# Loading two small matrices with two transfers on one queue instead of five on two

## The chip, the cores and the metric

The kernel runs on one core of a Trainium2 chip. The metric is device microseconds for one execution; lower is better. Before the change, three timed runs took 223.18, 223.17 and 222.88 us (median 223.17).

## The reference

Two blocks are chained. The first is an attention with sketched features: for each of 4 batches and 4 heads, queries, keys and values are 1088 tokens by 32, and two sketch matrices S1 and S2 (8 x 32 each) make the features.

```python
def phi(x):
    a = np.einsum('rd,bhsd->bhsr', S1, x)
    b = np.einsum('rd,bhsd->bhsr', S2, x)
    return np.einsum('bhsi,bhsj->bhsij', a, b).reshape(*x.shape[:-1], r * r)
q_p, k_p = (phi(q), phi(k))
kv = np.einsum('bhsf,bhsd->bhfd', k_p, v)
num = np.einsum('bhsf,bhfd->bhsd', q_p, kv)
den = np.einsum('bhsf,bhf->bhs', q_p, np.sum(k_p, axis=2))[..., None] + 1e-06
x = num / den                      # then (B,H,S,D) -> (B,S,H*D)
```

The second block turns x into a phase, `theta = x @ w_theta`, mixes `x*cos(theta)` and `x*sin(theta)` along the tokens with two 1088 x 1088 matrices (w_tok_r, w_tok_i), adds x to get u, and returns `u + relu(u @ w_ch)`. S1, S2 and the w matrices arrive as 8-byte floats, which the kernel unpacks itself.

## The kernel before

**Stages.** Tokens lie in chunks of 128 partitions. Keys, queries and values of a batch are one tile each: 128 rows of 4608 bytes, 576 KB, loaded by one transfer on SyncE's queue (SP in the profile, `load`, line 677). For each batch the kernel forms sums of key products (`key_sums`: keys are split into a short rounded part, `hf`, and a rest; matrix products of both are summed on TensorE), key features and their products with the values (`kfeatures`), and a normalising chain (`chain`). For three of the four batches the sums also need a second copy of the keys (line 723, the tile that the profile also calls `big<-k_l`), onto which GpSimd's queue adds the rounded part by an accumulating transfer (`join`, line 398, `big<-hf`). The token mixing, in which w_tok's 17 slabs of 1088 KB come in one after another (line 649), fills most of the second half of the run.

In what follows k0, k1, q0, k2, kh1, q1, k3 are the first seven of these 576 KB loads in the order in which SP issues them: keys of batches 0 and 1, queries of batch 0, keys of batch 2, the second copy of batch 1's keys, queries of batch 1, keys of batch 3. "The first join" is the accumulating transfer onto kh1, and "the rest products" are the TensorE instructions that read its result.

**What sets the order.** The kernel records some thousand operations, each with its engine and its buffers, and issues them in one order written out as a table of numbers (`ORDER`, lines 29 to 67). Each engine executes its own in that order. TensorE's list holds a fixed number of dummy products on a tile `idle` (line 435, `spin`), so that it isn't idle while it waits.

**Completion semaphores.** The transfers that SP and ScalarE (ACT) issue take eight completion semaphores in turn, and a transfer whose turn comes round again waits until the one that held that semaphore eight places earlier has landed. The built program shows this as waits on DMAHW0 to DMAHW7: in the program before, k2 is the ninth such transfer and waits for k0.

**The small matrices.** S1 and S2, transposed, are one input `s_t` of 32 rows by 16 eight-byte words (128 bytes a row); S2 is also an input `s_2` of 8 rows by 32 words. They go to the tile `st` of 128 partitions, `s_t` four times, once for each head's 32 partitions. Line 455 issues one transfer per copy, two on ACT's queue (line 464) and two on SP's (line 465); line 457 brings `s_2`, on SP's queue. All of them wait for a memset of `st` on VectorE (DVE, line 463).

**Who needs them.** ACT makes the upper words (`sp<-st`, line 471) after it has squared and summed k0 (line 702). DVE unpacks the rest (lines 477 to 480), takes a maximum (line 513), and by way of TensorE and ACT (`scaled`, lines 525 to 527) gets the scaled matrices that it rounds (`rounded`, `s<-sm`). Between these steps DVE also works on the keys: the rounded part of k0 (`hf`, line 388), its rest (line 384), then the rounded part of k1, which the first join adds.

Of the kernel before, what the change touches and what calls it, by code (L numbers as in the profile page):

```python
# [26 lines left out]
TINY = 2.0**-60  # L27
UP = 256.0
ORDER = """
    0 1 36 12 13 4 10 11 139 14 54 58 59 39 55 15 16 5 60 8 140 61 62 63 64 65 66 67 68 69 56 85 19 133 17 152  # L30
    18 127 37 70 20 41 89 57 71 72 21 22 73 91 74 75 80 81 23 128 134 82 76 297 94 153 90 24 25 3 92 299 29 245
    238 239 93 249 83 129 154 130 26 300 135 155 77 95 298 96 42 97 98 131 136 99 100 101 78 40 180 181 156 86
    295 146 137 32 296 158 147 33 251 254 255 301 102 87 141 48 49 34 7 51 50 38 52 79 174 232 302 159 132 256
    252 138 113 114 103 104 105 115 106 107 108 109 110 111 193 197 53 142 44 160 175 112 88 143 118 176 119 332
    333 161 162 9 226 120 121 27 186 144 233 145 35 122 187 257 258 199 352 123 259 260 261 2 124 354 28 84 125
    262 305 177 182 183 303 273 6 165 250 148 149 30 227 150 335 253 126 167 43 334 188 347 274 275 189 221 412
    416 336 417 116 117 348 418 276 419 420 413 414 169 168 415 190 178 421 422 222 202 223 423 203 204 205 166
    206 173 207 315 424 304 208 311 45 425 327 194 151 224 228 263 426 427 306 353 240 316 184 264 265 47 428
    157 163 229 164 319 429 171 430 241 431 432 46 328 433 307 195 308 309 234 179 434 342 323 329 185 324 320
    441 310 321 322 191 448 266 267 268 192 269 270 437 312 31 438 200 330 435 442 271 436 443 230 444 445 439  # L40
    331 337 235 236 446 523 440 519 520 338 339 451 452 447 521 455 457 524 525 458 449 522 526 450 515 516 517
    209 382 198 231 201 242 518 527 246 172 464 463 459 460 461 465 528 529 466 530 456 247 453 454 237 248 243
    462 272 472 531 340 532 533 313 467 341 534 468 244 471 349 372 170 535 344 473 314 469 210 211 212 536 213
    474 214 215 216 217 537 480 544 373 374 343 345 218 219 220 481 482 538 540 539 545 541 546 547 548 542 551
    549 543 559 550 196 470 552 346 553 355 475 362 554 566 350 558 555 477 560 561 562 351 357 317 356 564 556
    568 563 483 569 567 476 278 557 358 359 570 363 484 574 576 485 279 565 280 479 478 572 577 629 630 631 571
    365 281 583 578 360 606 573 607 580 282 364 608 283 284 384 632 361 367 369 633 634 584 407 277 285 609 225
    610 611 368 486 318 579 392 383 366 370 371 286 660 661 662 409 656 663 657 658 659 288 408 652 653 385 375
    376 654 575 581 585 397 586 410 411 582 587 635 636 386 637 638 394 588 291 293 393 287 395 396 655 664 377
    378 380 379 381 289 290 612 398 589 590 591 592 487 387 400 388 390 402 294 639 665 666 667 668 488 640 403  # L50
    669 670 671 389 391 489 672 673 825 490 491 404 399 405 678 401 492 493 494 406 495 676 674 325 326 679 828
    496 497 503 718 719 720 509 675 721 714 715 716 717 710 711 712 292 823 713 824 677 680 857 641 853 822 722
    681 642 723 643 593 498 682 724 683 684 725 726 727 728 686 729 730 731 734 644 732 736 685 735 687 688 499
    500 689 693 695 691 737 645 613 614 615 616 617 618 619 620 696 646 594 690 701 733 621 738 739 827 740 692
    741 697 698 702 595 856 703 694 742 699 704 705 802 803 501 744 783 784 785 804 743 765 707 792 767 700 805
    806 807 756 786 787 788 768 758 706 769 708 747 770 749 793 808 759 760 750 510 504 826 751 794 795 809 796
    797 798 762 855 745 761 746 748 752 753 754 774 502 596 622 709 852 755 764 766 819 757 623 881 789 790 771
    763 820 839 772 840 773 851 841 842 829 843 879 821 914 511 512 810 799 844 845 848 882 791 868 869 513 846
    775 811 776 777 778 624 597 849 854 850 877 858 870 878 847 871 872 873 647 779 780 781 895 883 916 598 782
    880 896 884 859 860 897 625 915 874 919 875 626 505 898 899 861 900 901 902 903 506 507 815 862 863 876 904  # L60
    908 864 917 920 936 937 508 909 830 831 865 866 800 867 816 921 514 938 832 833 834 922 927 835 836 837 838
    939 599 923 924 926 940 928 929 953 930 627 918 952 801 600 941 601 885 628 925 886 887 888 889 890 891 892
    893 894 812 813 814 648 649 650 912 651 942 943 944 931 817 954 818 910 932 965 913 975 966 905 906 933 934
    948 602 935 603 955 956 957 604 605 949 958 945 959 960 950 946 961 962 963 947 976 977 978 979 907 964 985
    967 968 969 970 951 986 980 971 911 972 973 987 988 981 982 983 974 984 989 991 990 992 993 994 996 995 997
    998
"""
WARM = 0
FILL = 5.0
# [250 lines left out]
def kernel(  # L320
# [12 lines left out]
    B, _, NC, H, D = q.shape  # L333
    S, DM = out.shape[1], out.shape[2]
    R = s_2.shape[0]
# [34 lines left out]
    op, buf = L.op, L.buf  # L370
# [4 lines left out]
    V, A, G, T, SY = nc.vector, nc.scalar, nc.gpsimd, nc.tensor, nc.sync  # L375

    def fixed(shape, dt, name):
        b = Buf(None, shape, dt, name)
        n = math.prod(shape) * WORD[dt]
        b.ap = view(const.tile([P, (n + 3) // 4], F32, tag=name, name=name), shape, dt)  # L380
        return b

    def tt(eng, o, a, b, f):
        eng.tensor_tensor(out=o, in0=a, in1=b, op=f)  # L384

    def ts(o, a, s1, op0, s2=None, op1=None, eng=None):
        kw = {} if op1 is None else {"op1": op1}
        (eng or V).tensor_scalar(out=o, in0=a, scalar1=s1, scalar2=s2, op0=op0, **kw)  # L388

    def stt(o, a, s, b, op0, op1, eng=None):  # L390
        (eng or V).scalar_tensor_tensor(out=o, in0=a, scalar=s, in1=b, op0=op0, op1=op1)  # L391
# [8 lines left out]
    def vop(n, fn, w, r, two=False, lk=0):  # L400
        op("V", dve2(n) if two else dve(n), fn, w, r, lk=1 if two else lk)
# [46 lines left out]
    NS = 2 * R + D  # L448
    sp = fixed((2, NS), F32, "sp")
    wide = s_t.dtype != F32  # L450

    def read_heads(E, i0, i1):
        dst = st() if wide else sp()[:, 0]
        for i in range(i0, i1):
            E.dma_start(dst[i * D:(i + 1) * D, 0:2 * R], s_t.rearrange("d t r -> d (t r)"))
        if i1 == H:
            E.dma_start(dst[0:R, 2 * R:NS], s_2)

    if wide:
        st = fixed((NS,), I64, "st")  # L460
        y = fixed((NS,), I32, "sy")
        z = fixed((NS,), I32, "sz")
        op("V", 0.1, lambda: V.memset(st().bitcast(F32), 0.0), [st], [])
        op("A", 0.48 * 2, lambda: read_heads(A, 0, 2), [(st, 0)], [], fly=2.7)
        op("S", 0.5, lambda: read_heads(SY, 2, H), [(st, 1)], [], lk=3)

        def words():
            w = st().bitcast(I32).rearrange("p (n t) -> p n t", t=2)
            return w[:, :, 0], w[:, :, 1]

        op("A", 0.25, lambda: A.activation(sp()[:, 0], words()[1].bitcast(F32), AF.Prelu, scale=2.0**-112,
                                           alpha=-(2.0**32)), [(sp, 0)], [st])

        def unpack():
            wl = words()[0]
            x = sp()[:, 0].bitcast(I32)
            ts(x, x, 3, ALU.logical_shift_left)
            stt(x, wl, 29, x, ALU.logical_shift_right, ALU.bitwise_or)
            ts(y(), x, -(1 << 23), ALU.bitwise_and)
            ts(z(), wl, 0x1FFFFFFF, ALU.bitwise_and)  # L480

        op("V", 0.85, unpack, [(sp, 0), y, z], [st], lk=2)
        op("A", 0.25, lambda: A.activation(sp()[:, 1], z(), AF.Copy, scale=2.0**-52), [(sp, 1)], [z])
        vop(NS, lambda: tt(V, sp()[:, 1], sp()[:, 1], y().bitcast(F32), ALU.mult), [(sp, 1)], [y])
    else:
        op("V", 0.2, lambda: V.memset(sp(), 0.0), [sp], [])
        op("A", 0.4 * H + 0.4, lambda: read_heads(A, 0, H), [(sp, 0)], [], fly=2.0)

    def powers(mfn, m, n, name):

# [6 lines left out]
        def inv():  # L497
# [16 lines left out]
                                    op=ALU.max, apply_absolute_value=True), [m2], [(sp, 0)])  # L514
# [989 lines left out]
```

## Time and profile before

| | |
|---|---|
| median of three runs | 223.17 us (222.88 to 223.18) |
| profiled execution | 222.87 us |
| span in its profile (first to last instruction) | 221.1 us |
| TensorE busy | 212.9 us of the span (96%) |
| DVE, ACT, GpSimd busy | 164.4, 113.5, 43.1 us |
| granted TensorE clock | 1.000 |
| moved by DMA | 40.19 MB |

The page divides the span into slices and says how busy each engine was; "PE" is TensorE's products, "PEld" its weight loads. A line of the timeline gives the start, the time from the first start to the last end, the engine, the source line, what is written and read, how many instructions were merged, and in brackets how long the engine had been idle and who ended the idleness. SPq, ACTq and POOLq are the issuing of transfers, which isn't counted as busy time. The chain of waits follows the end of the run backwards, at each step to what released it.

### The profile page before, as it was taken

How to read it: one execution, taken by the hardware profiler on the slowest of the kernel's cores; microseconds unless marked ns; L12 is line 12 of the kernel's file. 1: busy time of each engine (PE TensorE's matmuls, PEld its weight loads, DVE VectorE, ACT ScalarE, POOL GpSimd, SP SyncE). 2: the span in 40 equal slices, each digit the busy share in tenths (PEclk: the TensorE clock that was granted, in tenths of full speed). 3: DMA queues.
4: the chain of work that ended last, by engine and by line, in shares of the span. 5: the costliest groups of instructions: out<-in, count | busy, mean ns of one | idle time of the engine just before them, and what ended most of it. 6: DMA issues, size and time to landing. Idle time of an engine off the chain costs nothing.

```text
span 221.1 us, 5087 instructions
## 1 busy us (share of the span) xinstructions
PE 212.9 (96%) x2065; PEld 160.7 (73%) x2065; DVE 164.4 (74%) x343; ACT 113.5 (51%) x232; POOL 43.1 (20%) x79
## 2 busy tenths in 40 slices
PE   7997899989999999999999999999999999999992
PEld 3786688867876666687666687669878778778791
DVE  1889788999898999999999959943699132237631
ACT  4779359889999799856671251358920000000000
POOL 1146523001000000101002560000244355130000
PEclk9999999999999999999999999999999999999999
DMA  5999999993617306959900993002099689962572
GB/s 161 359 402 356 403 423 359 426 388 104 231 31 249 129 8 217 354 233 335 313 6 8 177 165 62 0 3 36 9 185 173 107 146 152 171 93 44 87 114 56
DMA packets 27047, 40.19 MB, mean 182 GB/s; under 512 B 18320, under 2 KB 19344, under 8 KB 24848
## 3 DMA queue, kind: packets, MB, share of 16 engines
q1 hardware_dynamic: 22176, 30.29, 40.4%
q0 software_dynamic: 4752, 9.57, 24.4%
q8 instruction: 16, 0.26, 0.5%
q14 instruction: 7, 0.06, 0.1%
q10 hardware_dynamic: 96, 0.01, 0.0%
HBM read 28.07 MB, written 2.23 MB: 137 GB/s over the span
## 4 chain that ended last, share of the span: by engine, by line
PE 81%; DMA 11%; ACT 3%; SPq 2%; issue 1%; DVE 1%; ACTq 0%; POOLq 0%
PE ps L404 75%; DMA big<-k_l 5%; DMA big<-hf 5%; PE ps L1191 2%; PE ps L1158 2%; SPq L1286 2%; PE ps L1038 1%; ACT big L652 1%; PE ps L435 1%; DMA out<-g 1%; ACT big L650 0%; ACT big L1006 0%; ACT big L1041 0%; PE ps L795 0%; ACT g L1298 0%
## 5 line engine op out<-in xcount | busy, mean ns | idle before, releaser
L404 PE MATMUL ps<-big,zs 128*128 128x384 f32 (+4 forms) x366 | 101.9, 426 | 0.0
L404 PEld LDWEIGHTS ps<-big,zs 128*128 128x128 f32 x366 | 65.5, 190 | 26.8 <-DVE big L388 0.6
L1270 ACT COPY g<-ps 128x384 f32<-128x384 f32 (+1 forms) x6 | 2.8, 459 | 41.5 <-PE ps L404 41.5
L650 ACT ACTIVATE big<-zs 128x1088 f32<-128x1088 f32 x17 | 20.5, 1214 | 5.3 <-DMA zs<-w_tok 5.3
L384 DVE CUSTOM_DVE_ANT_0 big<-big,big 128x2176 uint16<-128x2176 uint16 x17 | 21.8, 1287 | 0.4
L652 ACT ACTIVATE big<-zs 128x1088 int32<-128x1088 uint32 (+1 forms) x18 | 20.8, 1171 | 0.4 <-DVE big L384 0.2
L391 DVE SCALAR_TENSOR_TENSOR big<-ps,even,big 128x256 f32<-128x256 f32 (+1 forms) x10 | 4.9, 492 | 13.5 <-PE ps L404 13.5
L1331 POOL DMA_DIRECT2D big<-big x8 | 9.5, 1502 | 27.2 <-DVE big L384 15.0
L1331 POOL DMA_DIRECT2D big<-zs x8 | 7.7, 1063 | 36.8 <-PE ps L404 33.9
L404 PE MATMUL ps<-big,big 128*32 128x32 f32 (+2 forms) x320 | 13.7, 220 | 0.8 <-DMA big<-hf 0.8
L384 DVE TENSOR_TENSOR zs<-ps,g 128x768 f32<-128x768 f32 (+2 forms) x20 | 12.3, 627 | 2.9 <-PE ps L1191 1.7
L404 PE MATMUL ps<-mf,big 128*128 128x96 f32 x72 | 14.4, 295 | 0.0
L404 PEld LDWEIGHTS <-hf 128*32 128x32 bf16 (+1 forms) x252 | 10.8, 99 | 4.3 <-issue 2.3
L435 PE MATMUL ps<-idle 128*128 128x384 bf16 x46 | 11.7, 383 | 1.3 <-POOL idle L437 1.3
L404 PEld LDWEIGHTS ps<-big,big 128*32 128x32 f32 (+1 forms) x320 | 10.1, 117 | 3.9 <-DMA big<-hf 1.1
L1298 ACT COPY g<-ps 128x128 f32<-128x128 f32 x2 | 0.5, 265 | 22.9 <-DMA out<-g 22.2
L388 DVE TENSOR_SCALAR big<-big 128x1088 int32<-128x1088 int32 x17 | 12.0, 720 | 0.0
L404 PEld LDWEIGHTS ps<-w,big 128*128 128x128 f32 x76 | 10.1, 191 | 2.2 <-ACT g L1298 1.2
L404 PE MATMUL ps<-w,big 128*128 128x128 f32 x76 | 10.8, 278 | 0.8 <-ACT g L1298 0.8
L384 DVE TENSOR_TENSOR g<-lv 128x768 f32<-128x768 f32 x12 | 11.0, 952 | 0.6 <-PE ps L1158 0.6
L391 DVE SCALAR_TENSOR_TENSOR g<-g,ps 128x384 f32<-128x384 f32 x12 | 6.5, 545 | 6.1 <-ACT g L1200 6.1
L404 PEld LDWEIGHTS ps<-mf,big 128*128 128x128 f32 x72 | 10.9, 191 | 0.0
(195 smaller groups left out, 388.9 us busy)
## 6 DMA issues: line engine op xcount, KB each, us to landing
zs<-w_tok SPq DMA_DIRECT2D x17, 1088.0 KB, 6.6
big<-k_l SPq DMA_DIRECT2D x7, 576.0 KB, 6.8
big<-q_l SPq DMA_DIRECT2D x4, 576.0 KB, 11.0
big<-v_l SPq DMA_DIRECT2D x4, 576.0 KB, 15.0
big<-big POOLq DMA_DIRECT2D x8, 272.0 KB, 4.8
big<-zs POOLq DMA_DIRECT2D x8, 272.0 KB, 4.1
zs<-big POOLq DMA_DIRECT2D x8, 272.0 KB, 5.2
big<-hf POOLq DMA_DIRECT2D x3, 576.0 KB, 10.4
```

Of the source, the lines that this page charges most:

```text
L384: eng.tensor_tensor(out=o, in0=a, in1=b, op=f)
L388: (eng or V).tensor_scalar(out=o, in0=a, scalar1=s1, scalar2=s2, op0=op0, **kw)
L391: (eng or V).scalar_tensor_tensor(out=o, in0=a, scalar=s, in1=b, op0=op0, op1=op1)
L404: T.matmul(o, lhs, rhs, start=start, stop=stop, skip_group_check=True)
L435: T.matmul(nowhere(), idle()[:, 0:P], idle(), start=True, stop=True, skip_group_check=True)
L650: op("A", 0.22 + n * 0.0009, lambda: A.activation(dfn(), words_of(raw(), n)[1].bitcast(F32), AF.Prelu, scale=2.0**-112, alpha=-(2.0**32)), ...
L652: op("A", 0.22 + n * 0.0009, lambda: A.activation(stp(), words_of(raw(), n)[0].bitcast(U32), AF.Copy, scale=2.0**-29), [stp], [raw])
L1158: T.transpose(tr()[:, i * P:(i + 1) * P], qp()[:, i * H + 2 * n:i * H + 2 * n + 2].rearrange("p h i j -> p (h i j)"), ident())
L1191: T.transpose(x()[:, i], xs()[:, off + i * P:off + (i + 1) * P], ident())
L1270: op("A", act(w), lambda: A.copy(u(), yp()[:, :w]), [uT], [yp])
L1286: SY.dma_start(out[b, t0 - o:t0 + w, f * SQ:(f + 1) * SQ].rearrange("(c j) i -> j c i", j=SQ), ot()[f * SQ:(f + 1) * SQ, :o + w].rearrange ...
L1331: op("G", 1.05, lambda i=i: G.dma_start(dst[0](i), x[0](i), accum_op=ALU.add), [dst[1](i)], [x[1](i)], chan=ADD_FLY3)
```

## The change

Both inputs come on ACT's queue: one transfer writes all 128 partitions from `s_t`, with a source pattern that goes over the 32 rows four times, and one brings `s_2`. SP issues none of them. The recorded operations are one fewer, so the table of the order is numbered anew.

```diff
-    def read_heads(E, i0, i1):
+    def read_small():
         dst = st() if wide else sp()[:, 0]
-        for i in range(i0, i1):
-            E.dma_start(dst[i * D:(i + 1) * D, 0:2 * R], s_t.rearrange("d t r -> d (t r)"))
-        if i1 == H:
-            E.dma_start(dst[0:R, 2 * R:NS], s_2)
+        A.dma_start(dst[:, 0:2 * R],
+                    s_t.rearrange("d t r -> d (t r)").partition_broadcast(H))
+        A.dma_start(dst[0:R, 2 * R:NS], s_2)
...
-        op("A", 0.48 * 2, lambda: read_heads(A, 0, 2), [(st, 0)], [], fly=2.7)
-        op("S", 0.5, lambda: read_heads(SY, 2, H), [(st, 1)], [], lk=3)
+        op("A", 0.48 * 2, read_small, [st], [], fly=3.0)
```

In the built programs, each engine's list of instructions is the same before and after, in the same order and with the same number of dummy products, but for these transfers: ACT issues two before and two after, SP issues three fewer. What SP's and ACT's transfers wait for follows the new turns of the eight completion semaphores: k2, kh1 and q1 wait for none, and k3 is the first that waits for k0.

## Prediction

> **What bounds the kernel now.** I read the chain of waits first. Its pieces in order of time (start, us, what):
>
> ```profile
> 0.73 3.90 DMA big<-k_l
> 4.63 0.02 issue
> 4.64 0.33 SPq L677
> 4.97 0.04 issue
> 5.02 7.90 DMA big<-k_l
> ...
> 13.51 10.94 DMA big<-hf
> 24.45 0.04 issue
> 24.49 2.31 PE ps L404 x66
> ...
> 165.14 44.37 PE ps L404 x188
> ```
>
> From 24.49 us on nearly all of it is TensorE work, which the change leaves as it is. Before that it is a row of transfers: k0; then SP, which may issue k2 only when k0 has landed; kh1, issued right after; then the first join, which needs kh1. So the stage to look at is the first 24.5 us, and the question is how much sooner the rest products can start. The list of waits from 60 us on shows TensorE waiting 1.2 us in all, at the very end: what is gained at 24.49 us should last.
>
> The timeline of the first 14 us shows what the edit touches (start, duration, engine, line):
>
> ```profile
> 0.98 0.86 ACTq L455 DMA_DIRECT2D st<-s_t  x2
> 1.16 0.88 SPq L455 DMA_DIRECT2D st<-s_t  x2
> 2.08 0.37 SPq L457 DMA_DIRECT2D st<-s  x1
> 2.49 0.35 SPq L677 DMA_DIRECT2D big<-k_l  x1
> 5.81 0.23 ACT L471 ACTIVATE sp<-st 128x48 f32<-128x48 f32 x1
> 7.64 1.17 ACT L702 ACTIVATE big<-big 128x1152 f32<-128x1152 f32 x1 [0.77 <-DMA big<-k_l]
> 12.37 0.19 DVE L388 TENSOR_SCALAR s<-sm 128x48 f32<-128x48 f32 x1 [0.44 <-ACT sm L527]
> ```
>
> SP spends 1.16 to 2.49 us on small transfers, so k1 is issued at 2.49. ACT then waits for k1 (0.77 us), and DVE waits 0.44 us for ACT. TensorE's own timeline shows what stands ahead of the rest products:
>
> ```profile
> 21.84 0.22 PE L404 MATMUL ps<-g,big 128*32 128x64 f32 x1 [1.14 <-issue]
> 22.60 1.14 PE L435 MATMUL ps<-idle 128*128 128x384 bf16 x6
> 24.49 0.70 PE L404 MATMUL ps<-big,big 128*32 128x32 f32 x58 [0.76 <-DMA big<-hf]
> ```
>
> The six dummy products end at 23.74 us, and 0.76 us passes until the join has landed. This is the second limit: however early the join lands, the rest products can't start before TensorE has come through its list.
>
> **The change, step by step.**
>
> 1. *SP's issues.* Three go (0.41, 0.41 and 0.37 us). k1 moves from 2.49 to about 1.15. Issues come some 0.4 us apart, so q0 falls at 1.55 (before 2.89), k2 at 1.95 (4.64), kh1 at 2.35 (5.02), q1 at 2.75 (5.66). k2 gains most because its semaphore is fresh; k3 now waits for k0 and still goes at 4.64, not 6.13.
>
> 2. *Landings.* The DMA view, asked about one issue at a time, gives 3.9 us to landing for k0, 5.1 for k1, 6.4 for q0, 6.8 for k2, 7.9 for kh1 and 8.7 for q1, that is at 4.63, 7.6, 9.3, 11.4, 12.9 and 14.4. The steps between are 3.0, 1.7, 2.1, 1.5 and 1.5 us. The last two are the pace of a queue that is never empty (576 KB in 1.46 us is 404 GB/s). The long ones are times when it ran dry: the windows 4 to 5 and 7 to 8 us moved 157 and 304 GB/s, 12 to 13 us 436. With five loads queued from 2.75 us on, four steps of 1.46 behind 4.63 put kh1 at 10.5; I add 0.5 us for the small transfers, as the packet records show them between 3.7 and 4.3 us, and get 11.0, 1.9 sooner.
>
> 3. *The first join.* It needs kh1 and k1's rounded part. DVE ends that at 10.62 + 0.86 = 11.48, in a run of work that k0's landing starts and that has no wait over 0.2 us from 5.94 on, so it stays. The join waited 0.60 us from kh1's landing to its issue (12.91 to 13.51); from 11.48 that gives 12.1, 1.4 sooner. Its flight of 10.94 us is far longer than the 4.8 us of the join at 52 us, when little else moves, because it shares the engines with the loads; the same loads stand around it after the change, so I keep it: landing at 23.05. Bounds: 4.8 and 12.4 us (the old landing).
>
> 4. *ACT.* It still issues two, at 0.98 and about 1.40. No row shows the repeating source; between 0.37 us (8 rows) and 0.41 us (32 rows), and 0.33 to 0.43 us for 128-row loads, I take 0.41. Even four times 0.41 would end ahead of k0's square (4.65), before which ACT is idle 1.28 us. `s_t` should land as it did, 3.8 us after its issue, at 4.8. `s_2` is another matter: it used to be ahead of k1 on SP's queue and is now issued behind k1's issue on another. I let it wait for one load, 1.40 + 3.8 + 1.46 = 6.65. Bounds: 5.2 (no wait) and five loads, 12.5. At 6.65 `sp<-st` starts 0.84 us late. ACT is then free for k1's square at 6.88 + 0.84 = 7.72, with k1 landed; q0's square follows after 1.17 + 0.22 us, at 9.11 instead of 9.29, since q0 has landed too. So ACT is 0.18 us ahead at the scaled matrices. With `s_2` at 5.2 it would be ahead by more than DVE's 0.44 us of waiting.
>
> 5. *DVE.* Unpacking `sp` began at 7.11; `sp<-st` at 6.65 ends at 6.88, so nothing is lost. At 12.37 DVE gains the 0.18 us (between 0 and 0.44). From there it has no gap until 24.42 us, and feeds TensorE; ACT's 1.11 us wait for TensorE at 16.58 and TensorE's wait for k3 (landed at 15.7) move with them or go. I therefore move TensorE's 23.74 by 0.18 to 23.56.
>
> 6. *The sum.* The rest products start at the later of 23.05 and 23.56, not at 24.49: 0.93 us sooner. Behind them come the same TensorE, ACT and DVE instructions; later transfers, in a queue that is 1.9 us ahead, cover that. The profiled execution, 222.87 us (span 221.1 and 1.77 around it), becomes 221.94; the median lies 0.30 higher, so 222.24. A measurement of this kernel can tell about 0.2% (0.45 us) from no change.
>
> **A rule to weigh.** The packet records show some 210 small packets, rows and completions, done over all 16 DMA engines between 3.71 and 4.30 us, 13 an engine. The Trainium skill (DMA: Bandwidth & Descriptors, "Why a DMA increments its semaphore by 16 and not by 1") states that a transfer is spread over the largest number of engines, up to 16, that divides the slowest dimension of both its patterns. By that rule the repeating source, whose slowest dimension is 4, would run on 4 engines, and the sum would be that of rival B; no transfer of this trace has such a source.
>
> **The rivals.**
>
> - *A: more is gained.* TensorE stands still for 1.14 us ahead of 21.84 with no wait that the profile shows. If that falls elsewhere, TensorE's list is through before 23 us and the join decides, at 23.05 or, with a shorter flight, near 22: 1.4 to 2.4 us, 221 to 221.7 on the scale of the median. For: no semaphore holds it. Against: nothing in the edit reaches it.
> - *B: the gain is eaten by a crowded small transfer.* The repeated `s_t` runs on few engines. 13 packets took 0.59 us an engine; 33 would take 1.5, so `s_t` lands about 0.9 us later, at 5.7, and `s_2` behind it at 7.5. `sp<-st` ends at 7.75, DVE unpacks 0.55 us late, ACT is 1.7 us late, and the scaled matrices come 0.7 us late: TensorE is through its list at 24.44, the join long landed. Gain 0.05, 223.1.
> - *C: hidden anyway.* The join's flight grows by what its issue gains, since more is queued ahead of it: it lands at 24.2 or later. Gain 0.2 or none, 223.0. Against: its share of the queue isn't new, all loads are earlier alike.
> - *D: slower.* `s_2`, alone on ACT's queue, waits until most of what SP has queued is through. It decides from a landing at 7.5 on: each us beyond delays ACT's `sp<-st`, behind it k1's square, DVE's unpacking and rounding, and with them TensorE, one for one. One or two loads more, 9.0 to 10.4, give 1.5 to 2.9 us: 224.6 to 226. For: SP issued at most one load ahead of the small ones before, now six by 3 us. Against: ACT's packets ran as soon as k0's were done (3.7 us), side by side with SP's.
> - *E: it doesn't do what it says:* the loads land no earlier, because the dry spells come from the memory and not from late issues. Then only ACT's and DVE's fractions remain: 223.1.
>
> **How the numbers follow.** Forecast 0.50 (222.2, from 221.8 to 222.7 by the bounds of step 5), A 0.10, B 0.15, C 0.06, D 0.14, E 0.05. The range of 8 in 10 takes in the forecast, B, C, E and the nearer half of A: 221.3 to 223.4. Faster by over 0.2% (under 222.72): forecast and A, 0.60. Within 0.2%: B, C and E, 0.26. Slower: D, 0.14.
>
> **What would show it.** In the profile after, k1's issue at about 1.15, k2's near 2, kh1 landed by 11.0 (step 2; at 12.9 E is right); the join issued at 12.1 and landed at 23 (at 24.2 C); `sp<-st` at 6.65 with a wait on `st` (at 5.8 step 4 was too careful, at 7.5 it is B, later D); the rest products at 23.56, led by the dummy products with no wait on `big<-hf`. The prediction is wrong if the rest products start earlier but the time doesn't follow: then something between 24.5 and 50 us doesn't hang on them.

## The result, and the profile after

The changed kernel takes 229.34 us (median of 6, 228.81 to 229.59); the kernel before took 223.02 us beside it. The ratio is 1.028 [1.0261, 1.0299]: 2.8% slower, where 222.2 us was forecast and 223.4 was the upper end of the range. The profiled execution took 228.81 us, with a span of 227.0 us against 221.1, so nearly all of the 6 us can be looked for in its trace. (Ratios leave disturbed executions out; the profiles of E6, E14, E15 and E16 below are of disturbed ones, and only positions and local values are read from them.)

The chain of waits of the changed kernel, in order of time (start, us, what), answers to the one of before:

```profile
2.16 9.66 DMA st<-s
12.93 1.28 DVE big L383
14.95 2.62 PE ps L403 x100
...
29.87 2.24 PE ps L403 x66
...
170.88 44.36 PE ps L403 x188
```

The row of key loads and the first join are gone from it. What now holds everything is the small transfers' semaphore: 9.66 us from `s_2`'s issue to its landing at 11.82. The rest products start at 29.87, not 24.49, and the last long piece of TensorE is late by 5.7 us (170.88 against 165.14): what is lost in the first 30 us stays lost.

The timeline of the first 18 us of the changed kernel:

```profile
0.98 1.14 ACTq L453 DMA_DIRECT2D st<-s_t  x1
2.16 0.34 ACTq L455 DMA_DIRECT2D st<-s  x1
2.75 0.49 SPq L720 DMA_DIRECT2D big<-k_l  x1
11.47 0.33 SPq L646 DMA_DIRECT2D zs<-w_sq  x1
11.91 0.24 ACT L468 ACTIVATE sp<-st 128x48 f32<-128x48 f32 x1 [6.08 <-DMA st<-s]
14.25 0.28 PE L403 MATMUL ps<-big,big 128*32 128x32 f32 x8 [5.18 <-DVE big L383]
17.04 1.04 POOL L397 DMA_DIRECT2D big<-hf  x1 [1.97 <-DVE sm L387]
```

SP does what was intended: kh1 is issued at 2.75 instead of 5.02 (and lands at 11.0 instead of 12.9). But ACT stands 6.08 us in front of `sp<-st`, DVE behind it, TensorE idles 5.18 us, and the join is issued at 17.04, 3.5 us later than before, though kh1 has by then lain there for six microseconds. SP stands still as well: the load `w_sq`, the tenth transfer of the two queues, takes the semaphore that `s_t` holds and is issued at 11.47 us, right behind the landing of `s_t` (11.45), where it went at 6.62 before. The chain of waits does not pass through it.

TensorE pays twice. Its work on the first slice's differences, 132 products from 14.25 us, takes 6.13 us; before, the same work took 3.91. The windows of TensorE (stretch, length, busy with the number of products, granted clock, DMA share, GB/s), after and then before:

```profile
9.07:14.25 5.18, 0.00 (x0) 1.00 1.01 379
14.25:20.38 6.13, 6.13 (x132) 0.51 1.02 381
```

```profile
9.17:13.08 3.91, 3.85 (x133) 1.00 1.00 388
```

Having idled for 5.18 us, TensorE runs at a granted clock of 0.51 for the next 6 us. So at the end of this work it is 20.38 - 13.08 = 7.30 us late. Of that 1.9 us come back by 29.87: the stall of 1.14 us and the wait of 0.76 us for the join, which the kernel before had there, don't occur.

### The profile page after: what moved, and what is told of

It reads as the page before. It is cut to its first block, busy times and chain, and to the rows that moved or that the text cites. A ratio compares the mean times of both kernels' runs of the same rounds, so it can differ in the third digit from the quotient of the medians.

```text
span 227.0 us, 5081 instructions
## 1 busy us (share of the span) xinstructions
PE 214.6 (95%) x2065; PEld 162.4 (72%) x2065; DVE 164.4 (72%) x343; ACT 113.7 (50%) x232; POOL 43.8 (19%) x79
## 4 chain that ended last, share of the span: by engine, by line
PE 86%; DMA 5%; ACT 3%; DVE 2%; SPq 2%; issue 1%; ACTq 0%
PE ps L403 77%; DMA st<-s 4%; PE ps L1188 2%; PE ps L1155 2%; PE ps L1035 2%; PE ps L434 2%; SPq L1283 2%; PE ps L792 1%; ACT big L649 1%; DMA out<-g 1%; DVE big L383 1%; ACT big L647 0%; ACT big L1003 0%; ACT big L1038 0%; ACT g L1295 0%
```

## The experiments

Two questions came out of this. Why did the small transfers land at 11.8 us? And, from the first four runs on, a second one: why is a kernel no faster whose small transfers land in time *and* whose loads come early?

### The late landing

In the trace's semaphore record a plain `s_t` on ACT's queue has 16 updates (in the kernel before from 4.20 to 4.81 us); here it has five, one at 2.21 us, when its issue had just ended, and four singly, at 7.56, 9.16, 10.23 and 11.45. Read as 12 of the 16 counts at once and one for each engine at work, it ran on four engines with 32 rows each; the rule that the prediction weighed (the Trainium skill, DMA: Bandwidth & Descriptors, "Why a DMA increments its semaphore by 16 and not by 1") is borne out. The packet records of ACT's queue run from 5.32 to 11.34 us. Of these 148 packets some 60 are through by 5.80; from then on an engine does one small packet about every 0.20 us, in turn with the packets of SP's loads (4608 bytes, 0.18 to 0.19 us each). Theory 1: few engines, and there one row of the small transfer per packet of the loads. Theory 2: ACT's queue as such comes late when SP has many loads queued. A third, that a transfer on four engines is slow by itself, is tested along.

**E1, four plain transfers, all on ACT's queue.**

```diff
-        A.dma_start(dst[:, 0:2 * R], s_t.rearrange("d t r -> d (t r)").partition_broadcast(H))
+        for i in range(H):
+            A.dma_start(dst[i * D:(i + 1) * D, 0:2 * R], s_t.rearrange("d t r -> d (t r)"))
```

> As after, but s_t comes by four plain transfers of 32 rows, all on ACT's queue, then s_2. Theory 1 (the repeating source puts 32 rows on each of 4 engines, and there each small packet alternates with one 0.18 us packet of a load): now 13 or so small packets on each of 16 engines, so st is complete near 6.5 us, at most 7.5, and the time is 222 to 223.5. Theory 2 (ACT's queue as such is served late behind SP's five loads, whatever the number of engines): st complete at 11 or later, 229 or more.

223.95 us, ratio 1.0037 [1.0014, 1.0061]. ACT's line:

```profile
7.98 0.24 ACT L468 ACTIVATE sp<-st 128x48 f32<-128x48 f32 x1 [1.73 <-DMA st<-s]
```

ACT's queue, with everything on it, gives its data 3.9 us sooner than in the changed kernel. It is no full test of theory 2, though: its five transfers make k2 wait for k0 again (issued at 4.42), so SP has fewer loads queued while the small ones run.

**E2, one plain transfer of 128 rows** (the input is laid out with its 32 rows four times), and **E3, one transfer for everything** (one input of 128 rows of 384 bytes holds both matrices).

```diff
-        A.dma_start(dst[:, 0:2 * R], s_t.rearrange("d t r -> d (t r)").partition_broadcast(H))
-        A.dma_start(dst[0:R, 2 * R:NS], s_2)
+        A.dma_start(dst, s_t)          # E3; E2 keeps s_2's transfer
```

> As after, but the input s_t holds the 32 rows four times, so that one plain transfer of 128 rows brings them; s_2 follows. Theory 1: 8 rows and a completion on each of 16 engines, ACT's issue back to 0.4 us, st complete near 6.2, sp<-st by 6.5, and the time 0.5 to 1.2 us under before: 221.8 to 222.6. Theory 2: as after, 229.

> s_t and s_2 laid side by side in one input of 128 rows by 384 bytes (zeros where nothing stands), one plain transfer on ACT's queue. Theory 1: 8 rows and a completion on each engine, nothing behind them, st complete before k0's square ends (5.8), time 221.7 to 222.4. Theory 2: st complete after 10 us, 228 or more.

E2: 223.74 us, 1.0034 [1.0014, 1.0055]; E3: 223.76 us, 1.004 [1.0019, 1.0061], `sp<-st` at 5.68 with no wait. ACT's line in E2:

```profile
6.36 0.25 ACT L467 ACTIVATE sp<-st 128x48 f32<-128x48 f32 x1 [0.53 <-DMA st<-s]
```

The loads are as early as in the changed kernel and the small data on ACT's queue are in time, so theory 2 falls here. With 8 rows on each engine all of a plain `s_t` runs between 3.66 and 4.26 us, as the first rows of the repeating one did; its landings are at 4.73 (E2) and 4.67 (E3).

**E4, the changed kernel's two transfers on SP's queue,** behind k0's issue and ahead of k1's; the repeating source stays.

```diff
-        A.dma_start(dst[:, 0:2 * R], s_t....partition_broadcast(H))
-        A.dma_start(dst[0:R, 2 * R:NS], s_2)
+        SY.dma_start(dst[:, 0:2 * R], s_t....partition_broadcast(H))
+        SY.dma_start(dst[0:R, 2 * R:NS], s_2)
```

> The two transfers of after, the repeating source among them, but on SP's queue, between k0 and k1. On one queue they stand in line and don't alternate with the loads. Theory 1: 33 packets on 4 engines cost well under 1 us, st complete by 5.8, k1 issued near 2.7, time 222 to 223. Rival (4 engines alone make it slow, 33 packets at the 0.19 us each that after shows): st complete after 10 us and k1 held back on those engines as long, time over 228.

223.47 us, 1.0022 [1.0001, 1.0042]; `sp<-st` at 5.73 with no wait. Four engines are enough where the loads' packets are queued behind: on SP's own queue the rows run one after the other between 3.8 and 4.4 us and alternate with nothing; they have landed at 4.67. So four engines are not slow by themselves.

**E5, 64 rows repeated twice,** so that by theory 1 two engines carry 64 rows each (the input is laid out with its rows twice).

```diff
-                    s_t.rearrange("d t r -> d (t r)").partition_broadcast(H))
+                    s_t.rearrange("d t r -> d (t r)").partition_broadcast(2))
```

> The changed kernel, with an input of 64 rows (the 32 rows twice, laid out on the host) that the transfer repeats twice, not four times. Theory 1 (the repeat's count sets how many DMA engines carry the transfer, and each carries its rows one by one between the packets of the loads): 2 engines with 64 rows each, at the 0.19 us a row that the changed kernel showed: landing at 5.3 + 65 x 0.19 = about 17.6 us instead of 11.8, and TensorE's first products on its data 5.8 us later: 233 to 236. Rival theory 2 (the transfer is late because ACT's queue comes after SP's, whatever its engines): 229.3, as the changed kernel.

233.11 us, 1.0413 [1.0352, 1.0475]: slower again, as theory 1 says, but the landing came at 14.3 us and not at 17.6. The windows of its whole core (the last two columns are DMA share and GB/s) tell why:

```profile
11.00:12.00 1.00, 0.00 (x0) 0.00 (x0) 0.00 (x0) 0.00 (x0) 0.00 (x0) 1.00 1.06 421
12.00:13.00 1.00, 0.00 (x0) 0.00 (x0) 0.00 (x0) 0.00 (x0) 0.00 (x0) 1.00 0.47 181
13.00:14.00 1.00, 0.00 (x0) 0.00 (x0) 0.00 (x0) 0.00 (x0) 0.00 (x0) 1.00 0.06 18
```

The core stands still, and the loads run dry at 12.5 us, because the tenth transfer of the two queues, SP's `w_sq`, waits for the semaphore that `s_t` holds (it is issued at 14.17). From 7 us up to there the two engines did 10 to 13 small packets in each microsecond, 0.15 to 0.2 us for one on an engine; with no load beside them the last 36 went in under a microsecond. That is theory 1 with its other half shown: the price is the alternation and not the row. The other part of the distance to 17.6 is the start, where here too the first rows came faster (29 packets between 5.3 and 6 us).

**E6, TensorE kept busy during its wait,** with 14 f32 dummy products put in front of it.

```diff
+        calls.append(0)
+        if len(calls) == 20:
+            f = idle().bitcast(F32)
+            for _ in range(14):
+                T.matmul(nowhere()[:, 0:GW // 2], f[:, 0:P], f, start=True, stop=True, ...)
```

> The changed kernel, with 14 more dummy products of TensorE (f32, 192 columns, some 0.32 us each, 4.5 us in all) in the 5.2 us in which it waits for the small transfers' data. Theory C (part of the 6 us lost is TensorE's clock, which was granted at 0.72 in the 10 us behind its wait): TensorE's work from its first product on that data to the end of the dense run takes 3.9 to 4.2 us, not 6.1, and 1 to 2.2 us are won: 227.1 to 228.3. Rival: the slow stretch is not the clock but the data or the instruction fetch behind the wait: 229.3. What I can't exclude: with the clock held, TensorE meets its instruction fetch again, which takes back up to 1 us.

The clock held (1.00 from 14.5 to 18.3 us) and the same work took 3.76 us instead of 6.13, so the clock did cost 2.4 us there. The time did not follow, and the expectation missed: 230.84 us, 1.0339 [1.0305, 1.0372], slower than the changed kernel's 1.028. Its trace has two stalls without a wait that the changed kernel has not, 1.08 us ahead of 29.12 and 1.72 us ahead of 37.85. Nor was the clock won over the whole run: the mean granted clock of E6's six executions is 0.977 to 0.985, that of the changed kernel's six 0.974 to 0.983. The stalls lead to the second question.

### Where the early loads' gain goes

In E2, E3 and E4 the rest products start at 24.15, 23.82 and 23.31 us; the kernel before started them at 24.49, and 23.56 was forecast. (E1, whose k2 waits for k0, starts them at 24.73.) Yet all are 0.2 to 0.4% slower than before, and above the times expected of them. TensorE's timeline in E3:

```profile
15.97 0.23 PE L403 MATMUL ps<-big,big 128*32 128x32 f32 x4 [0.89 <-issue]
21.99 0.22 PE L403 MATMUL ps<-g,big 128*32 128x64 f32 x1 [0.68 <-issue]
27.96 0.21 PE L403 MATMUL ps<-sq,sm 32*32 32x16 f32 x3 [0.86 <-issue]
```

"Issue" is idle time that no semaphore explains; before had one such stall, 1.14 us ahead of 21.84. I numbered TensorE's instructions in the trace (weight loads, products and semaphore instructions, from 0). The three stalls stand ahead of numbers 449, 705 and 961, and the one of before ahead of 705: always 256 apart. The DMA view has a queue of kind "instruction" (q8), with packets of 16 KB, and 16384 / 256 = 64 bytes. The packets lie like this (us on the profile's clock):

| kernel | packet | then starts number | idle ahead of it |
|---|---|---|---|
| before | 12.98 to 13.90 | 449 at 15.35 | none |
| | 19.57 to 20.54 | 705 at 21.84 | 1.14 |
| | 25.42 to 26.40 | 961 at 27.70 | none |
| E3 | 13.44 to 14.48 | 449 at 15.97 | 0.89 |
| | 19.69 to 20.57 | 705 at 21.99 | 0.68 |
| | 25.55 to 26.55 | 961 at 27.96 | 0.86 |

In each of these stalls the first instruction of a block starts 1.3 to 1.5 us after a packet's end, and each packet of the table starts 3.3 to 4.2 us after TensorE entered the block before. This gives theory F: TensorE's instructions come in blocks of 256; in this stretch the fetch of a block begins after the one before it has been entered, about 6 us pass from there until it can start, and TensorE is often through 256 instructions of small products sooner. The Trainium skill (Runtime: NRT & Kernel Launch, "Instruction fetch mechanics") describes blocks of 16 KiB, 256 instructions, fetched ahead by the sequencer on a DMA queue of its own, and calls the cost at a boundary mostly hidden. The size agrees with the trace; hidden it is not, by the 0.7 to 1.1 us in the table. Rivals: G, the stalls belong to those products; H, what follows waits for other data.

In before, E1 to E5 and the changed kernel the span ends 193.4 to 193.7 us after number 961 starts (27.70 and 221.1 before; 33.31 and 227.0 after; 27.96 and 221.6 in E3). The whole comparison can be read there.

**E7 and E8: the same products at other numbers.** E3, with one wide dummy product of the first group replaced by 25 narrow ones (48 instructions more), and with three replaced by 83 (160 more).

```diff
-    first = op("P", 3.6, lambda: [spin() for _ in range(11)], [nowhere], [idle])
+    def pad():
+        T.matmul(nowhere()[0:32, 0:8], idle()[:, 0:32], idle()[:, 0:8], start=True, stop=True, ...)
+    first = op("P", 3.6, lambda: [spin() for _ in range(10)] + [pad() for _ in range(25)], [nowhere], [idle])
```

> The kernel with one plain small transfer, with one wide dummy product of TensorE's first group replaced by 25 narrow ones (8 columns): 48 more TensorE instructions ahead of all work, about the same time. Theory F (TensorE gets its instructions in blocks of 256 that are fetched by DMA, and under full DMA queues a block can start no sooner than 5.9 to 6.3 us after the one before it): the stalls stay ahead of TensorE's records 449, 705 and 961, so they move to products that stand 48 records earlier in the work; the boundary at record 193 falls ahead of the dense run of small products, so that each later block holds more work than 6 us can feed: 1.5 to 3.3 us slower than the same kernel without the padding (223.8), 225.3 to 227. Rival theory G (the stalls belong to those products: their data or the clock): the stalls stay ahead of the same products, the time stays at 223.8.

> The same, with three wide dummy products replaced by 83 narrow ones: 160 more TensorE instructions ahead of the work. Theory F: the boundaries fall at products that stand 160 records earlier, so the dense run lies within a block whose fetch began at about 5 us; the three stalls of 2.4 us shrink or go: 0.5 to 1.1 us faster than without the padding, 222.7 to 223.3. Theory G: the same three stalls, 223.8.

E7: 227.49 us, 1.0184 [1.014, 1.0229]. E8: 226.04 us, 1.0139 [1.012, 1.0159]. E8's stalls:

```profile
11.89 0.19 PE L403 MATMUL ps<-big,big 128*32 128x32 f32 x1 [0.99 <-issue]
18.22 0.22 PE L403 MATMUL ps<-big,big 128*32 128x32 f32 x2 [0.83 <-issue]
26.12 0.73 PE L403 MATMUL ps<-big,big 128*32 128x32 f32 x61 [1.03 <-issue]
32.20 0.42 PE L403 MATMUL ps<-g,big 128*32 128x64 f32 x14 [1.11 <-issue]
```

The products behind the stalls are others than in E3, and their numbers are 449, 705, 961 and 1217; in E7 they are 449 and 961 (0.77 and 2.96 us). In all twenty traces (the two kernels and E1 to E18), the 33 stalls of TensorE over 0.3 us in the first 70 us that the profile puts down to "issue" all stand at 193 + 256 n. G is refuted. The sizes were wrong: E7 lost a little more than expected (behind its stall of 2.96 us the granted clock was 0.50 from 28.3 to 31.7 us), and E8 did not gain. Its 83 narrow products took 2.29 us where I had reckoned 1.0, and a fourth stall appeared: with more instructions to fetch in the same time none of the places tried for the boundaries was good.

**E9 and E10: the 160 instructions ahead of the kernel before and of E4** (the same edit as E8).

> The kernel before (five small transfers) with the same 160 more TensorE instructions. Theory F: the stall of 1.14 us ahead of 21.84 goes, but the rest products still wait for the first join at about 24.45, so at most 0.3 us is gained: 222.8 to 223.2, the wait on the join then over 1.5 us. Theory G: the stall stays, 223.1.

> The kernel with both small transfers (the repeating source too) on SP's queue behind k0, with the same 160 more TensorE instructions. Theory F: the two stalls of 1.8 us shrink or go, 0.1 to 0.9 us faster than without the padding (223.47): 222.6 to 223.4. Theory G: unchanged, 223.5.

E9: 229.34 us, 1.0203 [1.0171, 1.0236]; E10: 227.75 us, 1.0196 [1.0173, 1.0218]. Both expectations missed, in part for E8's reason: in E9 the narrow products took 2.38 us, and the first transposes behind them 0.85 us for three instead of 0.49 in E8. The stalls stand at 705, 961 and 1217 in E9, at 705 and 1217 in E10. The other part is the clock. In both, behind the stall of 1217 (1.11 us in E9, 1.39 in E10), it was granted at 0.50 for 6.8 us (from 33.6 to 40.4 us in E9). The 256 instructions from 1217 took 12.41 us in E9 and 10.05 in E8, which kept its full clock behind a stall of 1.11 us at the same place; what decides that is not shown.

**E11 and E12: fewer dummy instructions,** one f32 product of 192 columns for two bf16 ones of 384, in E4 and in the kernel before.

```diff
-    idle = fixed((GW,), BF16, "idle")
+    idle = fixed((GW // 2,), F32, "idle")
...
-        T.matmul(nowhere(), idle()[:, 0:P], idle(), start=True, stop=True, skip_group_check=True)
+        T.matmul(nowhere()[:, 0:GW // 2], idle()[:, 0:P], idle(), start=True, stop=True, skip_group_check=True)
```

> Both small transfers on SP's queue behind k0, and TensorE's dummy products halved in number: one f32 product of 192 columns for two bf16 products of 384, about the same time, 20 instructions fewer ahead of record 193 and some 15 fewer from there to record 961. Theory F (instructions are fetched in blocks of 256 that can't start under 5.9 to 6.3 us apart): fewer instructions to feed, so 0.3 to 0.7 us faster than with the bf16 dummies (223.47): 222.7 to 223.2. Rival: the fetch takes back what it may, whatever the count: 223.5.

> The kernel before with the same halved dummy products. Theory F: its one stall of 1.14 us goes or shrinks, but the rest products still wait for the first join at 24.45: 0 to 0.3 us faster than before, 222.7 to 223.1. The distance to the same kernel with both small transfers on SP's queue then tells what the earlier loads are worth when fewer instructions have to come: 0.2 to 0.6 us by theory F, none by its rival.

E11: 224.0 us, 1.0034 [1.0009, 1.0058]; E12: 223.55 us, 1.0015 [0.9992, 1.0038]. Nothing was gained, and nothing was tested: in the trace an f32 product is two weight loads and two products, so TensorE has 4176 instructions where it had 4172. The stalls stay at 705 and 961.

**E13 and E14: 224 instructions fewer.** In E4 and in the kernel before, seven of nine chunks of the first slice's difference products are left out.

```diff
                 def two(c=c):
+                    if b == 0 and 0 < c < NC - 1:
+                        return
                     x = rows_(rc(), c)
```

> Both small transfers on SP's queue behind k0, and seven of the nine chunks of the first slice's difference products left out (the dense run of small products from 9.04 us): 224 TensorE instructions fewer between its records 193 and 449, in about 1 us of its time. Part of the computation is left out. Theory F (the instruction fetch holds TensorE from 10 to 28 us): without the fetch as a limit the rest products start when the first join lands, near 23, with no stall behind them: 0.9 to 1.7 us faster than the kernel before with the same products left out, 221.3 to 222.2. Rival theory H (the earlier loads buy nothing here, whatever the fetch, because what follows waits for other data): as the kernel before with the same products left out, within 0.3 us.

> The kernel before with the same seven chunks left out. Both theories: the rest products wait for the first join as before, landing at 24.45, with a longer wait on it (over 1.5 us) and no stall of 1.14 us ahead of 21.84: 222.7 to 223.3.

E13: 223.14 us, 0.9976 [0.9943, 1.001]; E14: 225.62 us, 1.0036 [0.9998, 1.0074]. E13 is ahead by 0.6%, near theory F's size, but the intervals overlap, both times lie above what was expected, E13 still meets one fetch (1.50 us ahead of 705), and E14's TensorE idles 2.91 us at the join. The pair decides nothing.

**E15 and E16: 15 dummy products left out** between 11 and 27 us, in E4 and in the kernel before.

```diff
     def spin():
+        calls.append(0)
+        if 20 < len(calls) <= 35:
+            return
```

> Both small transfers on SP's queue behind k0, and 15 of TensorE's dummy products (those between 11 and 27 us) left out: 30 instructions fewer from record 193 to record 961, the computation whole. Theory F: at some 21 to 23 ns an instruction (256 in 5.5 to 6 us) 0.4 to 0.7 us faster than with them (223.47): 222.7 to 223.1. Theory H: no change, 223.5; if TensorE's clock falls for want of the dummies, slower.

> The kernel before with the same 15 dummy products left out. The rest products wait for the join at 24.45 as before; behind them, theory F: 0 to 0.5 us faster than before (222.6 to 223.1), since record 961 came just as its block was there; theory H: no change, 223.1.

E15: 228.12 us, 1.0159 [1.0089, 1.0229]; E16: 230.2 us, 1.0186 [1.0128, 1.0244]. Both missed: the dummies hold the clock. In E16 TensorE waits 1.83 us for the join, and the mean granted clock of its six executions is 0.923 to 0.970 (E15's: 0.920 to 0.983), where the kernel before had 0.973 to 1.000 beside them.

**E17 and E18: the pair once more, with both disturbances taken away.** Five chunks are left out (160 instructions fewer, and the boundaries clear of the join), E17 is E3, E18 the kernel before with 12 dummy products more at its wait for the join.

```diff
+                    if b == 0 and 0 < c < 6:       # both
+                        return
...
-        T.matmul(nowhere(), idle()[:, 0:P], idle(), ...)
+        for _ in range(13 if len(calls) == 30 else 1):      # E18
+            T.matmul(nowhere(), idle()[:, 0:P], idle(), ...)
```

> One plain small transfer, early loads, and five of the nine chunks of the first slice's difference products left out (part of the computation): 160 TensorE instructions fewer, so that record 449 is reached near 18.3 us and record 705 falls among the rest products at about 24.2, later than its block needs. Theory F: no stall over 0.4 us from 10 to 30 us, the rest products start at the join's landing near 22.7: 221.3 to 222.3, 0.8 to 1.6 us faster than the kernel before with the same chunks left out. Theory H (the earlier loads buy nothing, whatever the fetch): within 0.4 us of it.

> The kernel before with the same five chunks left out, and 12 more dummy products of TensorE where it waits for the first join, so that its clock holds. Both theories: the rest products start when the join has landed, near 24.5, at full clock: 222.6 to 223.3.

E17: 223.22 us, 1.0003 [0.9977, 1.0029]; E18: 225.14 us, 1.0075 [1.0052, 1.0098]. The intervals are apart. The chains of waits, E17 first:

```profile
12.06 11.50 DMA big<-hf
23.60 2.31 PE ps L403 x66
...
35.61 3.66 PE ps L403 x62
...
40.75 3.39 PE ps L403 x110
```

```profile
13.16 11.46 DMA big<-hf
24.66 2.31 PE ps L404 x66
...
36.84 3.66 PE ps L404 x62
...
41.99 3.39 PE ps L404 x110
...
50.68 1.38 issue
```

The join is issued 1.10 us earlier with early loads and takes as long (11.50 and 11.46), the rest products start 1.06 us earlier, and the lead is 1.24 us at the 110 products near 41: it lasts, since no stall over 0.35 us stands between. H is refuted, for kernels with these chunks left out. The rest of the distance of the two spans (220.9 and 223.4) is E18's stall of 1.38 us at number 1729, which is no merit of the loads. Neither time came out as low as expected (221.3 to 222.3, and 222.6 to 223.3); E17, with work left out, is no faster than before. Its rest products start 0.89 us earlier than in the kernel before (23.60 against 24.49), but at its last long piece only 0.42 us are left (164.72 against 165.14): TensorE idles 0.28 us in front of number 961, and the nine products around number 1729 take 1.34 us instead of 1.13, so even there the block boundaries take about half of it.

No complete kernel tried here is faster than the kernel before.

## Why the prediction was wrong

1. *SP's issues* were right: q0 at 1.63, k2 2.10, kh1 2.75, q1 3.28, k3 4.57, within 0.6 us of what was written.
2. *Landings* were right: 11.0 for kh1 was forecast and measured. Rival E is refuted. (The small transfers' landings belong to step 4.)
3. *The first join* was wrong in the changed kernel, where it is issued at 17.04 and not at 12.1, since DVE's rounded part of k1 came late. With the small data in time it is issued at 11.73 (E2), 11.67 (E3) and 12.09 (E4), and its flight stays near the 10.94 us that were kept: 11.1 to 11.7 us in E2 to E4, 11.50 and 11.46 in E17 and E18. In E3 it landed at 23.05, as forecast, so rival C does not hold.
4. *ACT* is the step that failed, in the words "`s_t` should land as it did, 3.8 us after its issue, at 4.8". It landed at 11.45, and `s_2`, behind it on the same engines, at 11.82 where 6.65 was forecast: inside the bounds (5.2 and 12.5), but near the end that was not chosen. The sentence on `s_2`, "I let it wait for one load, 1.40 + 3.8 + 1.46 = 6.65", was about right by itself: behind a plain `s_t` it landed at 6.27 (E2), and in the changed kernel four of its eight single landings came between 6.33 and 7.30; the other four each came 0.4 us behind one of `s_t`'s, as on the engines that carry its rows. The mechanism was named as rival B, few engines, and its result under D, slower; what was missing is that they are one. B priced a row at 0.59 / 13 = 45 ns, from rows of before that came in a burst at 3.7 us. Beside five queued loads that price held only for the first rows, to 5.80 us; from there a row waits for a load's packet, and the last engine's some 28 packets at 0.20 us took the 5.5 us to 11.34. The repeating source also took 1.14 us to issue, where 0.41 was set.
5. *DVE and TensorE* follow from 4. "DVE gains the 0.18 us" became a wait of 5.07 us. D's rule, one for one from a landing at 7.5 us on, gives 223.1 + 4.3 = 227.4 us for 11.82. Not foreseen was the clock: 2.2 us for idling 5.2 us, which makes up the rest to 229.3.
6. *The sum* has a second fault that step 4 hides. With the small data in time the rest products start at 23.31 to 24.15 us (E2 to E4), around the forecast (23.56). But "behind them come the same TensorE, ACT and DVE instructions" left out that TensorE's instructions have to arrive. The stall of 1.14 us, which was left in place as unexplained, was the sign: TensorE was at its fetch limit before the change, 705 late and 961 just in time. The prediction said what would show this: the rest products earlier and the time not following.

Rival A, that this stall falls elsewhere, came about in the changed kernel, but only because TensorE was so late that its blocks were there. The chance of 0.14 for slower was too small because B and D had been priced as two separate mishaps.

What stays open: why a fetch begins 3 to 5 us after the block before is entered in these 35 us, and only 1.18, 1.12, 0.32 and 0.78 us after it for the blocks that the kernel before enters at 47.8, 55.5, 62.3 and 73.4 us. Later, among long products, a packet even comes ahead of that (at 117.18 us, with the next block entered at 122.21), so the entry that the trace shows is not itself what starts a fetch. The loads queued by SP are a likely reason for the late ones, but no run here took them away.

## What to carry to other kernels

Behind a first burst, a small transfer shared each DMA engine with the loads row by row: what counted is how many rows one engine gets, times the duration of one packet of the load beside it. Keep small data on all sixteen engines, or in the loads' own queue ahead of them, and give no repeating source to a queue that runs beside them. Where the profile shows idle time that nothing explains at equal distances in the instruction count, as here every 256, suspect TensorE's instruction fetch; data that come earlier then bought little or nothing, and added instructions cost time (E7 to E10), though dummy products that hold the clock earned theirs (E15, E16).

## What the runs showed of the hardware that was not expected

- A transfer with a source repeated four times took 1.14 us to issue on ACT's queue and 0.71 on SP's; a plain one of 128 rows took 0.43.
- Where TensorE stalled at a block of 256 instructions, or had it just in time, the block before had been entered 5.6 to 6.5 us earlier in before and E1 to E4 (4.3 to 8.7 us over all kernels). The packet itself took 0.9 to 1.1 us of that in before and E1 to E4.
- After 5.2 us of idling TensorE ran at a granted clock of 0.51 for 6 us (the changed kernel). Shorter stalls were followed by 0.50 as well: one of 2.96 us in E7 (for 3.4 us), of 1.11 and 1.39 us in E9 and E10 (for 6.8 us each); E8's of 1.11 us was not.
- An f32 product of 128 x 192 was two weight loads and two products in the trace (E6: 14 written, 28 recorded).
